# Moving the expert layers of two batches, a few loads and the tail of an mLSTM + mixture-of-depths kernel

## The chip, the cores and the metric

The kernel runs on one core of one Trainium2 chip. The metric is the device time of one execution in microseconds, lower is better. The engines are named as the profile names them: PE (matmuls, with its weight loads as PEld), DVE (vector), ACT (scalar, activations), POOL (GpSimd), and SP, which here only issues DMAs.

## What is computed

First an mLSTM cell over q, k, v of 4 batches, 8 heads, 768 tokens, 40 numbers per head. Its output, with the heads side by side, is x of 4 x 768 x 320, and goes into a mixture-of-depths layer: in each batch the 128 tokens with the highest scores go through two dense layers, the others pass unchanged.

```python
for t in range(S):                      # mLSTM, per batch and head
    m_new = np.maximum(f_gate[:, :, t] + m, i_gate[:, :, t])
    f_stab = np.exp(f_gate[:, :, t] + m - m_new)
    i_stab = np.exp(i_gate[:, :, t] - m_new)
    C = f_stab * C + i_stab * outer(vt, kt)
    n = f_stab * n + i_stab * kt
    y[:, :, t] = sigmoid(o_gate[:, :, t]) * (C @ qt) / max(abs(n @ qt), 1)
...
scores = np.einsum('bsd,d->bs', x, w_gate)
out = x.copy()
for b in range(B):                      # mixture of depths, capacity 128
    top_idx = np.argpartition(-scores[b], capacity)[:capacity]
    xe = x[b, top_idx]
    ye = np.maximum(xe @ w1, 0.0) @ w2  # 320 -> 1024 -> 320
    out[b, top_idx] = x[b, top_idx] + sigmoid(scores)[:, None] * ye
```

All of it is float32.

## The kernel before

The order of every engine's work is written out by hand in `_fast`; nothing is rescheduled, so each engine and each DMA queue does its instructions in the order of the program text. The sequence is cut into 12 steps n = 0 to 11: batch b = n // 3, and 256 tokens s = n % 3 of it. A step does the following.

- SP issues the loads of step n + 3 (`load`): v and k (`load_kv`, two DMAs of 160 KB each), q (one of 320 KB), and the output gate o of step n + 2 (`load_o`, four of 80 KB). The results of a step (x) are stored by `store`, two DMAs. The buffers of k, q and v go round by three. All of these DMAs are in one queue, SP's. Stores 0, 1, 2 are issued in step 4 and stores 3, 4 in step 5, between q and o of the loads; the weights w1 and w1c (the rows of w1 above 256) at the end of step 4's issues, w2 at the beginning of step 5's.
- `scores(n)` (line 297): 64 small matmuls k times q into the PSUM tile pS. `masked(n)` (line 303): DVE masks them into P.
- `fill` (line 562) repeats a dummy matmul twice, in steps 1 to 6.
- `widen(n+1)` (ACT, line 223) and `turn(n+1, "kT")`: PE transposes k of the next step (line 231), ACT copies it out of PSUM (line 233). `update(n+1)` (line 264) makes the contributions to the state C from k and the weighed v; `states` (DVE, lines 276 to 284) sums them. `weigh(n+2)` (POOL, line 243) multiplies v by the gates, two steps ahead.
- `read(n)` (line 319) multiplies q by the states; `turn(n+1, "qT")`; `attend(n)` (line 329) adds P times v. `divide(n)` (DVE, lines 338 to 343) makes y, `output(n)` (POOL, line 351) multiplies by the sigmoid of o into x, and `router(n)` (DVE, line 366) sums the scores of the tokens.

The mixture of depths runs between these. After a batch's last step, `spread` (line 394) lays all its scores along the free axis on all partitions; `ranks` counts for each token how many are greater, half by DVE (`greater`, line 406) and half by ACT (`signs`, line 411); `select` (DVE, line 445) makes a one-hot matrix of the ranks; `numbers` (PE, line 488) and `index` (DVE, lines 451 to 456) turn it into row numbers; `fetch` (POOL, line 494) gathers the 128 rows from `out` in HBM by an indirect DMA, so it waits until the stores of the batch have landed. `fetched` (PE, line 503) transposes the rows; `layer1` (lines 529 and 533, half of the 1024 columns per call, ReLU on ACT at line 535), `layer2` (line 545), `weighed` (ACT, line 550), and `add` (POOL, line 554), an indirect DMA that adds the result onto `out`.

In the kernel before, ranks and select of batch 0 are in step 5, with its fetch at the end of that step; `fetched(0)` and both halves of `layer1(0)` come at the end of step 6; `layer2(0)`, `weighed(0)` and `add(0)` in step 7. Batch 1 has ranks and fetch in step 7, `fetched` and `layer1` at the end of step 8, the rest in step 10. Batch 2 has ranks and fetch in step 10, `fetched` and its first half of layer1 in step 11, before `read`.

Batch 3 makes the tail. Its rows are not gathered from HBM: `picked` (lines 464 to 473) makes the one-hot matrix in float32, and PE multiplies x by it in three groups of columns (line 471). Four of the six score columns are compared early (`ranks_first`); the last two are spread by `spread(b, 4, 6, keep=True)`, which leaves them in PSUM, and compared there by DVE and ACT (`ranks_last`). `picked_numbers` (line 479) gets score, count and row number of the picked tokens by six float32 matmuls of 3 columns. A final matmul pg (line 678) sums flags that tell whether the fast path held.

PSUM is handed out in tiles by tag: "s" (pS, pB, a half of layer1) and pU each have one buffer of two banks, "h" (pH, pX) one, "t" (transposes, py, pi) two of one bank.

Of the kernel before, what the change touches and what calls it, by code (L numbers as in the profile page):

```python
# [9 lines left out]
FP = mybir.dt.float32  # L10
# [16 lines left out]
def _fast(ctx, tc, q, k, v, i_gate, f_gate, o_gate, w_gate, w1_in, w2_in, out):  # L27
# [49 lines left out]

    def load(n, between=()):

        if n < N:  # L80
            load_kv(n, v_t, v)
            load_kv(n, k_t, k)
            load_q(n)
        for i in between:
            store(i)
        if n <= N:
            load_o(n - 1)
# [199 lines left out]

    def scores(n):
        kT, qT = pending[n]["kT"], pending[n]["qT"]
        pS = ps_s.tile([128, 2, 2, NP, 64], FP, name="pS", tag="s")  # L290
        for c in range(2):
            for p in range(NP):
                for j in range(2):
                    for r in range(2):
                        e, o = slice(64 * j, 64 * j + D), slice(64 * r, 64 * r + 64)
                        t = slice(128 * c + 64 * r, 128 * c + 64 * r + 64)
                        PE.matmul(pS[o, j, c, p, :], kT[e, p, t], qT[e, p, t], start=True, stop=True)  # L297
        pending[n]["pS"] = pS
# [89 lines left out]

    def spread(b, r0, r1, keep=False):

# [5 lines left out]
        flat = pB.rearrange("p j t -> p (j t)")[:, 0:128 * w]  # L396
        if keep:
            return flat
        sb = mod.tile([128, 128 * w], FP, name=f"sb{w}", bufs=1)
# [28 lines left out]
    def ranks_last(b):  # L428
# [7 lines left out]
        DVE.tensor_scalar(out=part[:, 4:6], in0=part[:, 4:6], scalar1=0.5 * 255, scalar2=None, op0=OP.add)  # L436
        sb = spread(b, 4, 6, keep=True)
        for r in range(6):
# [20 lines left out]
    def picked(b):  # L459
# [7 lines left out]
        for j, pX in enumerate((ps_u.tile([128, 2, 512], FP, name="pU"), ps_h.tile([128, 2, 512], FP, name="pX", tag="h"),  # L467
                                ps_t.tile([128, 1, 512], FP, name="pX", tag="t"))):
            w = min(128, DM - 128 * j)
            for r in range(2 * NS):  # L470
                PE.matmul(pX[0:w, 0, 0:128], x[:, r, 128 * j:128 * j + w], sel[:, r, :], start=(r == 0), stop=(r == 2 * NS - 1))
            ACT.copy(out=d["xeT"][0:w, j], in_=pX[0:w, 0, 0:128])
        DVE.tensor_copy(out=d["xeT"][64:128, 2], in_=pX[0:64, 0, 0:128])

    def picked_numbers(b):
        x, d = x_t[b % 2], dep[b]
        pi = ps_t.tile([128, 3], FP, name="pi", tag="t")
        for r in range(2 * NS):
            PE.matmul(pi, d["sel_f"][:, r, :], x[:, r, DM:DM + 3], start=(r == 0), stop=(r == 2 * NS - 1))
        d["g"] = mod.tile([128, 1], FP, name="g")  # L480
# [34 lines left out]
    def layer1(b, f0):  # L515
# [5 lines left out]
        early, last = b < B - 2, b == B - 1  # L521
        if (early and f0 == 0) or (last and f0 > 0):
            ph = ps_s.tile([128, 2, 512], FP, name="ph", tag="s")
        else:
            ph = ps_u.tile([128, 2, 512], FP, name="pU")
# [54 lines left out]
    for n in range(N):  # L580
# [3 lines left out]
        given = late or n == 5  # L584
        if n == 5:
            SP.dma_start(out=w2, in_=w2_in.rearrange("(f p) d -> p f d", p=128))
        if n in (6, 9):
            store(n - 1)
        if n > 0:
            load(n + 3, {4: (0, 1, 2), 5: (3, 4)}.get(n, ()))  # L590
        if n == 4:
            SP.dma_start(out=w1, in_=w1_in[0:256, :].rearrange("(j p) f -> p j f", j=2))
            for i in range(2):
                SP.dma_start(out=w1c[64 * i:64 * i + 64],
                             in_=w1_in[256:DM, :].rearrange("p (f i e) -> p i f e", i=2, e=128)[:, i])
        if n in (7, 8, 10, 11):
            store(n - 1)
        scores(n)
        masked(n)
        if n == 0:  # L600
            update(0)
            load(3)
            states(0)
        if 0 < n < 7:
            fill(spare(n + 1)[:, 0], 2)
        if late:
            layer2(b - 2)
        if given:
            ranks(b - 1)
            select(b - 1)  # L610
        if late:
            weighed(b - 2)
        if n > 0 and (s == 0 or late or not more):
# [9 lines left out]
        if not more:  # L623
            sigmoid(n)
            gated(n)
            fetched(b - 1)
            layer1(b - 1, 0)
        read(n)
        if late:
            numbers(b - 1, spare(n + 1)[:, 1, 0:3])  # L630
        if n + 2 < N:
            weigh(n + 2)
        if late:
            fetch(b - 1)
        if n == 0:
            update(1)
            states(1)
        if more:
            turn(n + 1, "qT")
            sigmoid(n)  # L640
            if b > 0 and s == 0:
                dep[b - 1] = {"sb": spread(b - 1, 0, 2 * NS)}
        else:
            dep[b] = {"sb4": spread(b, 0, 4)}
            ranks_first(b)
        attend(n)
# [3 lines left out]
        if more:  # L650
            output(n)
        if n == 5:
            fetch(b - 1)
        if late:
            add(b - 2)
        if n == 0:
            tables()
        if n == 1:
            margins()
        if n in (6, 8):  # L660
            fetched(n // 4 - 1)
            layer1(n // 4 - 1, 0)
            layer1(n // 4 - 1, 4)
    b = B - 1
# [4 lines left out]
    store(N - 1)  # L669
    layer2(b - 1)  # L670
    picked(b)
    picked_numbers(b)
    weighed(b - 1)
    layer1(b, 0)
    add(b - 1)
    good = gate.tile([1, 1], I32, name="good")
# [362 lines left out]
```

## Time and profile before

| what | value |
|---|---|
| time, median of 4 runs | 178.08 us (176.32 to 179.85) |
| the profiled execution's own time | 176.32 us |
| its span, first to last instruction | 174.5 us |
| PE busy / weight loads | 150.6 us (86%) / 130.8 us (75%) |
| DVE, ACT, POOL busy | 92.8, 73.9, 68.8 us |
| granted TensorE clock, mean | 0.970 |
| DMA | 24.14 MB in 94104 packets, 88401 of them under 512 bytes |
| SP's queue | 69.2% of 16 engines' span |
| chain that ended last | PE 51%, DMA 18%, DVE 9%, issue 7%, POOL 6% |

The span is cut in the page into 40 slices of 4.36 us, with the busy share of each engine in tenths. A row of the timeline or of the chain begins with its start in us from the span's start and its length; `x16` is the number of instructions merged into it, and a bracket tells how long the engine was idle before it and what released it. The steps begin (first matmul of `scores`) at 12.91, 21.53, 28.74, 37.03, 46.02, 53.30, 62.72, 85.48, 97.31, 111.32, 119.44 and 131.26 us.

### The profile page before, as it was taken

What the parts mean: (1) busy time and instruction counts of PE and PEld (TensorE: products, weight loads), DVE (VectorE), ACT (ScalarE), POOL (GpSimd) and SP (SyncE); (2) the same over time, 40 slices, a digit from 0 to 9 for tenths busy, and PEclk for the clock granted to TensorE, in tenths of its full rate; (3) what the DMA queues carried; (4) which work ended last, traced back from release to release, by engine and by line L of the source; (5) the groups of instructions that cost most, each with busy time, mean ns of one, the idle gap of its engine ahead of it and who ended that gap; (6) DMA issues with size and microseconds to landing.
All of it is one profiled execution on the core that took longest, in us unless ns stands there. A gap on an engine that the chain in (4) does not pass through costs nothing.

```text
span 174.5 us, 6700 instructions
## 1 busy us (share of the span) xinstructions
PE 150.6 (86%) x2877; PEld 130.8 (75%) x2877; DVE 92.8 (53%) x252; ACT 73.9 (42%) x140; POOL 68.8 (39%) x89
## 2 busy tenths in 40 slices
PE   7969999899996978819999988999995999889930
PEld 7859899688985866808868977898694987678710
DVE  4676466486567996321196475185958756210000
ACT  0668464345459433320554553449343193121110
POOL 8045476745545336200721935671124712003030
PEclk9999999999999999996999999999999999996995
DMA  6999888898999789699989999997821603003003
GB/s 104 191 164 187 163 139 152 140 175 133 154 164 169 123 154 260 126 374 305 227 190 178 162 171 187 203 140 151 159 53 41 116 0 75 6 0 38 11 8 41
DMA packets 94104, 24.14 MB, mean 138 GB/s; under 512 B 88401, under 2 KB 93714, under 8 KB 94066
## 3 DMA queue, kind: packets, MB, share of 16 engines
q1 hardware_dynamic: 93104, 22.32, 69.2%
q0 software_dynamic: 720, 1.15, 4.1%
q8 instruction: 24, 0.39, 0.9%
q10 hardware_dynamic: 242, 0.17, 0.5%
q14 instruction: 14, 0.11, 0.2%
HBM read 19.04 MB, written 4.59 MB: 135 GB/s over the span
## 4 chain that ended last, share of the span: by engine, by line
PE 51%; DMA 18%; DVE 9%; issue 7%; POOL 6%; ACT 3%; ACTq 1%; SPq 1%; POOLq 0%; DVEq 0%
PE pt L231 8%; PE pU L264 7%; DMA xe<-out_dram,idx 6%; PE pH L329 5%; PE py L545 5%; DMA v<-in_v_dram 5%; PE pH L319 5%; PE pS L297 4%; PE pU L529 3%; PE ph L529 3%; POOL wv L243 3%; DMA k<-in_k_dram 3%; DMA out_dram<-yg,idx 2%; PE pB L394 2%; DMA i_sb<-in_i_gate_dram 2%
## 5 line engine op out<-in xcount | busy, mean ns | idle before, releaser
L243 POOL TENSOR_TENSOR wv<-v,cols 64x656 f32<-64x656 f32 x23 | 31.2, 1357 | 51.9 <-DMA v<-in_v_dram 47.4
L351 POOL TENSOR_TENSOR x<-y,o 128x320 f32<-128x320 f32 x24 | 20.5, 873 | 13.2 <-DVE x L384 5.0
L303 DVE TENSOR_TENSOR P<-pS,mask 128x1024 f32<-128x1024 f32 x12 | 14.6, 1217 | 13.9 <-PE pS L297 13.0
L235 ACT COPY qT<-pt 128x512 f32<-128x512 f32 x24 | 13.9, 633 | 18.6 <-PE pt L231 18.6
L545 PE MATMUL py<-w,hT 128*128 128x320 f32 x64 | 18.2, 437 | 0.0
L223 ACT COPY qw<-q 128x640 f32<-128x640 f32 x12 | 8.7, 722 | 21.5 <-DMA q<-in_q_dram 19.2
L231 PE MATMUL pt<-ident,k 128*128 128x128 f32 x96 | 14.2, 282 | 3.7 <-DMA k<-in_k_dram 3.1
L264 PE MATMUL pU<-wv,k 128*64 128x82 f32 x384 | 16.5, 237 | 0.1
L276 DVE TENSOR_TENSOR C<-pU,C 128x164 f32<-128x164 f32 x40 | 13.1, 328 | 6.6 <-PE pU L264 5.5
L329 PE MATMUL pH<-wv,P 128*64 128x82 f32 x384 | 16.3, 237 | 0.0
L554 POOL DMA_INDIRECT out_dram<-yg,idx x4 | 6.4, 1603 | 24.4 <-ACT yg L550 21.4
L264 PEld LDWEIGHTS pU<-wv,k 128*64 128x64 f32 x384 | 14.4, 137 | 2.1 <-issue 1.6
L366 DVE CUSTOM_DVE_ANT_0 scr<-x,wg 128x320 f32<-128x320 f32 x22 | 13.6, 616 | 4.2 <-POOL x L351 2.6
L329 PEld LDWEIGHTS pH<-wv,P 128*64 128x64 f32 x384 | 14.3, 136 | 1.8 <-issue 1.0
L231 PEld LDWEIGHTS pt<-ident,k 128*128 128x128 f32 x96 | 11.1, 145 | 5.8 <-PE pt L231 1.7
L545 PEld LDWEIGHTS py<-w,hT 128*128 128x128 f32 x64 | 11.8, 190 | 4.7
L319 PE MATMUL pH<-C,qT 40*64 40x41 f32 x704 | 14.0, 229 | 0.7 <-issue 0.7
L297 PE MATMUL pS<-qT,kT 40*64 40x64 f32 x768 | 13.9, 221 | 0.7 <-ACT qT L235 0.7
L319 PEld LDWEIGHTS pH<-C,qT 40*64 40x64 f32 x704 | 12.5, 134 | 2.0 <-issue 1.0
L297 PEld LDWEIGHTS pS<-qT,kT 40*64 40x64 f32 x768 | 12.3, 134 | 2.0 <-ACT qT L235 0.9
L233 ACT COPY kT<-pt 128x512 f32<-128x512 f32 x24 | 12.8, 586 | 1.8 <-PE pt L231 1.8
L231 PE MATMUL pt<-ident,qw 128*128 128x128 f32 x96 | 13.2, 279 | 0.4 <-DVE cols L216 0.4
(136 smaller groups left out, 223.5 us busy)
## 6 DMA issues: line engine op xcount, KB each, us to landing
k<-in_k_dram SPq DMA_DIRECT2D x24, 160.0 KB, 5.0
q<-in_q_dram SPq DMA_DIRECT2D x12, 320.0 KB, 5.7
v<-in_v_dram SPq DMA_DIRECT2D x24, 160.0 KB, 4.1
o<-in_o_gate_dram SPq DMA_DIRECT2D x48, 80.0 KB, 3.8
out_dram<-x SPq DMA_DIRECT2D x24, 160.0 KB, 2.8
w<-in_moe_w_dram SPq DMA_DIRECT2D x1, 1280.0 KB, 8.1
w<-in_moe_w_dram SPq DMA_DIRECT2D x1, 1024.0 KB
w1c<-in_moe_w_dram SPq DMA_DIRECT2D x2, 128.0 KB
```

The source lines that it names most:

```text
L231: PE.transpose(pt[:, p, :], src[:, c, 2 * p:2 * p + 2, :].rearrange("s j d -> s (j d)"), ident)
L235: ACT.copy(out=T.rearrange("e p (u t) -> e t p u", t=2)[:, c], in_=pt)
L243: (DVE if n == 0 and r else POOL).tensor_tensor(out=wv_t[n % 3][o, :, :, r], in0=v_t[n % NB][o], op=OP.mult, in1=cols[s][o, 0:2, b * H:b * ...
L264: PE.matmul(pU[64 * j:64 * j + 64, c, p], k_t[n % NB][:, c, 2 * p + j, :], wv_t[n % 3][:, c, 2 * p + j], start=True, stop=True)
L276: DVE.tensor_tensor(out=C, in0=src, in1=state[n, i], op=OP.add)
L297: PE.matmul(pS[o, j, c, p, :], kT[e, p, t], qT[e, p, t], start=True, stop=True)
L303: DVE.tensor_tensor(out=P.rearrange(flat), in0=pending[n].pop("pS").rearrange(flat), op=OP.mult, in1=mask.unsqueeze(1).to_broadcast([128, ...
L319: PE.matmul(g["pH"][64 * c:64 * c + 64, NP * j + p, r], g["qT"][e, p, t], state[n, 2 * c + r][e, p, :], start=(c, j) not in g["begun"], st ...
L329: PE.matmul(g["pH"][64 * c:64 * c + 64, NP * j + p], g["P"][:, j, c, p, :], wv_t[n % 3][:, c, 2 * p + j], start=(c, j) not in g["begun"], ...
L351: POOL.tensor_tensor(out=x.rearrange(order, j=2, d=D), in0=pending[n]["y"][:, r].rearrange("s (j p) d -> s j p d", j=2), in1=o.rearrange(o ...
L366: DVE.tensor_tensor_reduce(out=scr, in0=x[:, r, 0:DM], in1=wg, scale=1.0, scalar=0.0, op0=OP.mult, op1=OP.add, accum_out=x[:, r, DM:DM + 1])
L545: PE.matmul(d["py"], d["hT"][:, f, :], w2[:, f, :], start=(f == 0), stop=(f == NF - 1))
```

## The change

- Loads: store 0 goes to step 4, stores 1 and 2 into the loads of step 8 (step 5), behind v and k and ahead of q; w1 and w1c one step later, followed by stores 3 and 4; w2 one step later.
- Batches 0 and 1: `fetch(0)` moves from step 5 to step 6, behind `output`; `fetch(1)` stays in step 7 but behind `output(7)`, and `weigh(9)` comes behind it. `fetched` of both moves into the middle of `scores` of steps 8 and 9, `layer1` of both behind `masked` of those steps; `layer2(0)`, `weighed(0)` and `add(0)` from step 7 to step 8. The two halves of `layer1` of these batches change PSUM tiles. Step 7 gets a `fill`.
- Step 11: `fetched(2)` behind `read`, `layer1(2, 0)` behind `spread`.
- Tail: the last two score columns are copied to SBUF by ACT before they are compared; `picked` carries the three extra columns of x (score, count, row number) along in its third group of matmuls, and `picked_numbers` becomes one transpose of 3 partitions; `weighed(2)` and `add(2)` move up, and `layer1(3, 0)` comes ahead of `picked_numbers`.

```diff
-    def load(n, between=()):
+    def load(n):
         if n < N:
             load_kv(n, v_t, v)
             load_kv(n, k_t, k)
+            if n == 8:
+                store(1)
+                store(2)
             load_q(n)
-        for i in between:
-            store(i)
+        if n == 7:
+            store(0)
         if n <= N:
             load_o(n - 1)
...
-    def scores(n):
+    def scores(n, between=None):
...
         for c in range(2):
+            if c == 1 and between is not None:
+                between()
             for p in range(NP):
...
-    def spread(b, r0, r1, keep=False):
+    def spread(b, r0, r1):
...
-        if keep:
-            return flat
         sb = mod.tile([128, 128 * w], FP, name=f"sb{w}", bufs=1)
         ACT.copy(out=sb, in_=flat)
         return sb
...
-        sb = spread(b, 4, 6, keep=True)
+        sb = spread(b, 4, 6)
...
-            w = min(128, DM - 128 * j)
+            w = min(128, XW - 128 * j)
             for r in range(2 * NS):
                 PE.matmul(pX[0:w, 0, 0:128], x[:, r, 128 * j:128 * j + w], sel[:, r, :], start=(r == 0), stop=(r == 2 * NS - 1))
+            w = min(128, DM - 128 * j)
             ACT.copy(out=d["xeT"][0:w, j], in_=pX[0:w, 0, 0:128])
         DVE.tensor_copy(out=d["xeT"][64:128, 2], in_=pX[0:64, 0, 0:128])
+        d["three"] = mod.tile([128, 128], FP, name="three", bufs=1)
+        DVE.tensor_copy(out=d["three"][64:XW - 256], in_=pX[64:XW - 256, 0, 0:128])
     def picked_numbers(b):
-        x, d = x_t[b % 2], dep[b]
+        d, e = dep[b], slice(64, XW - 256)
         pi = ps_t.tile([128, 3], FP, name="pi", tag="t")
-        for r in range(2 * NS):
-            PE.matmul(pi, d["sel_f"][:, r, :], x[:, r, DM:DM + 3], start=(r == 0), stop=(r == 2 * NS - 1))
+        PE.transpose(pi, d["three"][e], ident[e, e])
...
-        if (early and f0 == 0) or (last and f0 > 0):
+        if (early and f0 > 0) or (last and f0 > 0):
             ph = ps_s.tile([128, 2, 512], FP, name="ph", tag="s")
...
-        if n == 5:
+        if n == 6:
             SP.dma_start(out=w2, in_=w2_in.rearrange("(f p) d -> p f d", p=128))
         if n in (6, 9):
             store(n - 1)
         if n > 0:
-            load(n + 3, {4: (0, 1, 2), 5: (3, 4)}.get(n, ()))
-        if n == 4:
+            load(n + 3)
+        if n == 5:
             SP.dma_start(out=w1, in_=w1_in[0:256, :].rearrange("(j p) f -> p j f", j=2))
...
+            store(3)
+            store(4)
...
-        scores(n)
+        scores(n, (lambda: fetched(n - 8)) if n in (8, 9) else None)
         masked(n)
...
-        if 0 < n < 7:
+        if 0 < n < 8:
             fill(spare(n + 1)[:, 0], 2)
-        if late:
-            layer2(b - 2)
+        if n in (8, 9):
+            layer1(n - 8, 0)
+            layer1(n - 8, 4)
+        if n in (8, 10):
+            layer2(n // 2 - 4)
...
-        if late:
-            weighed(b - 2)
+        if n in (8, 10):
+            weighed(n // 2 - 4)
...
             gated(n)
-            fetched(b - 1)
-            layer1(b - 1, 0)
         read(n)
...
-        if n + 2 < N:
+        if n + 2 < N and n != 7:
             weigh(n + 2)
-        if late:
-            fetch(b - 1)
+        if n == 10:
+            fetch(2)
...
         else:
+            fetched(b - 1)
             dep[b] = {"sb4": spread(b, 0, 4)}
+            layer1(b - 1, 0)
             ranks_first(b)
...
-        if n == 5:
-            fetch(b - 1)
-        if late:
-            add(b - 2)
+        if n in (6, 7):
+            fetch(n - 6)
+        if n == 7:
+            weigh(n + 2)
+        if n in (8, 10):
+            add(n // 2 - 4)
...
-        if n in (6, 8):
-            fetched(n // 4 - 1)
-            layer1(n // 4 - 1, 0)
-            layer1(n // 4 - 1, 4)
...
     layer2(b - 1)
+    weighed(b - 1)
     picked(b)
+    add(b - 1)
+    layer1(b, 0)
     picked_numbers(b)
-    weighed(b - 1)
-    layer1(b, 0)
-    add(b - 1)
```

## The prediction

> **What bounds the kernel now.** I read the page's slices first, then the chain of work that ended last, then the timeline around each long piece of that chain, with the SP queue beside it.
>
> The page's slices (4.36 us each) show what is scarce:
>
> ```profile
> PE   7969999899996978819999988999995999889930
> DVE  4676466486567996321196475185958756210000
> PEclk9999999999999999996999999999999999996995
> DMA  6999888898999789699989999997821603003003
> ```
>
> PE is full almost everywhere, and the DMA engines are full up to slice 27 (122 us): two resources are near their limit together. PE's hole is in slices 16 to 18, and its clock falls there and again in slice 36.
>
> The chain puts names on the holes (start, length, what ran):
>
> ```profile
> 71.41 6.09 DMA xe<-out_dram,idx
> ...
> 77.64 0.53 PE pX L503 x3
> ...
> 78.62 3.67 PE ph L529 x16
> ...
> 129.97 3.85 DMA xe<-out_dram,idx
> ...
> 154.56 1.51 PE pi L479 x12
> ```
>
> PE waits for the gather of batch 0 from 73.64 to 77.64, then runs layer1(0)'s first 16 matmuls in 3.67 us instead of the 2.05 of later ones. The chain holds few other waits of that size before the tail.
>
> The SP queue's timeline shows that it issues without a pause:
>
> ```profile
> 63.38 4.86 SPq L358 DMA_DIRECT2D out_dram<-x  x6
> 68.29 2.71 SPq L75 DMA_DIRECT2D o<-in_o_gate_dram  x4
> 71.04 1.26 SPq L592 DMA_DIRECT2D w<-in_moe_w_dram  x1
> 72.35 1.20 SPq L594 DMA_DIRECT2D w1c<-in_moe_w_dram  x2
> 73.59 0.69 SPq L586 DMA_DIRECT2D w<-in_moe_w_dram  x1
> 74.38 4.32 SPq L64 DMA_DIRECT2D v<-in_v_dram  x2
> ...
> 90.62 1.33 SPq L64 DMA_DIRECT2D v<-in_v_dram  x2
> ```
>
> v and k of step 8 leave at 74.38 to 82.24, behind six stores and both weights, and the loads of step 9 from 90.62. So a saving on PE is real only if the loads come as early.
>
> The tail, by the windows' rows (PE busy, PEld, DVE, ACT, POOL, granted clock, DMA):
>
> ```profile
> 154.00:156.00 2.00, 1.44 (x13) 1.44 (x13) 0.28 (x1) 0.19 (x1) 0.00 (x0) 1.00 0.00 0
> 156.00:158.00 2.00, 2.00 (x16) 2.00 (x16) 0.38 (x3) 0.59 (x2) 1.03 (x1) 0.82 0.00 0
> 158.00:160.00 2.00, 2.00 (x14) 1.51 (x13) 0.20 (x2) 0.34 (x1) 0.54 (x1) 0.50 0.48 37
> 160.00:162.00 2.00, 2.00 (x16) 2.00 (x15) 0.10 (x1) 0.25 (x1) 0.00 (x0) 0.83 0.31 53
> ```
>
> Right after the thin pi matmuls (3 columns each) the clock is halved for about 3.4 us (0.18, 0.50 and 0.17 of three 2 us windows are lost), while PE does layer1(3).
>
> **Part 1, batches 0 and 1 (steps 7 to 9).** Before, PE ends attend(6) at 73.64 and starts turn(10) at 112.42: 38.8 us. I rebuild this stretch with its own rows.
>
> Step 7, from 73.64: scores 1.09, fill 0.64 (new), turn k 1.02, update 1.28, read 1.07 give 78.7. Now numbers(1) needs DVE's select, and layer2(0), which gave it 4.5 us of cover, is gone: this is a new wait. DVE: y of step 6 ends at 75.21; from the start of P to the end of select took 5.34 us before (86.71 to 92.05), so select ends at 80.6 and PE stands about 2 us. Behind it wait turn q (1.02) and attend (1.29); with numbers 0.29, step 7 ends at 83.3. ACT meets the same time: widen(8) waits for q8 and the copies of turn k stand behind it. q8 now has two stores more in front, so it leaves near 74 and with the queue's median of 5.7 us lands at 79 to 80; that is level with select.
>
> The loads: SP ends q7's issue at 63.3. Store 0 takes 1.3, four o loads 2.7 to 4.1, v8 and k8 2.5 to 4, so k8 is issued by about 71.5 and lands (5.0) by 76, against a turn k at 75.4: 0 to 1 us, inside the 2 us wait above. Stores 1 and 2 land by about 77; fetch(0) goes at 77, after output(6), and takes 5.4 to 6.1 us: 82.5 to 83.2, in time for the transposes at 83.9. The 6 us gather is now under step 7.
>
> Step 8, from 83.3: scores with the three transposes inside 1.62, layer1 twice 2.05+0.65 less pipelining = 5.33, layer2 4.52: 94.8. The xeT copies (0.46 of PE idle before) lie under the second half of the scores. w1 leaves at 76 to 81; the nearest row is w2, 8.1 us to landing for more bytes, the low end a k load, 5.0: 81 to 89. I take 84, as w1 before was issued at 71.04 and in use by 78.62; it is needed at 84.9, so the bound of this cost is 0 to 4 us. The halves of layer1 change PSUM tiles: the second uses that of the scores, free after P (1.22), under the first half's 2.65; cost nothing, 1.2 without that cover.
>
> Then k9. The same items stand ahead of v9 in both orders (v8, k8, q8, o6, o7, stores 0 to 5, w1, w2), so the DMA work ahead of it is the same; only slack can go. The one slice below 8 there is slice 16 (69.8 to 74.2, "6"), some 1.7 us, and the six stores in a row left at SP's pace. I take 2 us; bounds 0 and 3. The second k9 load was issued at 93.1, now 91.1, and lands at 96.1 by the median 5.0. PE reaches it at 95.4 and stands 0.7. weigh(9) is now behind fetch(1) on POOL, and fetch(1) behind the landing of stores 3 to 5 (issued by 89, landed by 92): fetch 1.06 and weigh 2.6 end by 96, just under turn k. After k9: second half of turn 0.65, update 1.28, read 1.07, turn q 1.02, attend 1.29, and I keep the 0.67 us of unexplained idle in read(8): 102.1. Step 9: scores with transposes 1.62, layer1 5.33: turn(10) at 109.0. **Gain 3.4 us**; 1.4 with no slack, 4.1 with k9 no obstacle. Later loads move with v9 by the same 2 us and were early (k11 leaves at 111, is used at 125). add(0), 1.65 on POOL, and add(1) stay off the path.
>
> **Part 2, step 11.** Before, PE waited from 132.35 to 133.95 for the gather and 0.46 for the copies. Now read (1.07) and spread (1.09) come between. Next late is router(10): its scores are ready at 135.8, and half of spread's columns need them. PE then ends spread at 136.15, layer1 2.7, attend 1.3: 140.2 against 141.1. **Gain 0.9**; bounds 0.1 (all of spread waits) and 1.9 (no wait).
>
> **Part 3, the tail from the end of attend(11).** Before, 141.08 to the end of layer2(3) at 167.34: 26.3 us.
> Comparing from SBUF costs one ACT copy of 128x256 (0.37, L505's row; under 0.58, the row of 512 columns), under DVE's two 512-column comparisons (to 145.15); uncovered it would cost itself. ACT's three signs, which stood 2.61 us behind DVE's comparisons, now run beside them; a sign of 256 from SBUF lies between 0.47 and 0.72. Select is ready 1.7 us sooner, and PE's layer2(2) is late next, ending 7.57 us after attend (148.65 on the old scale) where picked began at 149.53. Picked takes 4.39; its 3 more columns ride in the third group. "three" is one small DVE copy (at most L473's 0.28), under layer1. layer1(3,0) then follows at once, since its first 16 matmuls need only copies already made: 2.70. pi is one transpose (between pg's 0.19 and the old 1.51; 0.2, it is nearest to pg), then a new wait: pg stands behind ACT's g and DVE's idx and flags, 0.75 (pi's end 156.06 to flags' end 156.72, and a semaphore), formerly under layer1; layer1(3,4) is queued behind it. pg 0.15, layer1 2.70, layer2 4.52. Sum 7.57+4.39+2.70+0.2+0.75+0.15+2.70+4.52 = 22.98. **Gain 3.3**, of which 1.7 is the halved clock, which I expect gone with pi's 1.5 us. Final weighed and add are unchanged, and add(2) moves away from them.
>
> The Trainium skill, "TensorE: Matmul & The Clock Gate" (Part 1), speaks against this last term: the clock halves after an idle window of about 3.4 us. Here PE was busy 1.44 of 2 us just ahead of the halving, with no gap over 0.9 us, so by that rule pi would not be the cause and might leave the slow stretch in place: the gain would be 1.6, not 3.3. I follow the row.
>
> **Sum.** 3.4 + 0.9 + 3.3 = 7.6 us. The profiled execution took 176.32 (span 174.5), so it becomes 168.7; it is the fastest of the four runs, 1.76 below their median of 178.08, and on that base the forecast is 170.5 us.
>
> **Rivals.**
> (a) The queue has no slack to give: part 1 gives 1.4 us when only k9 is late and about none with w1 at its late end; with 0.5 the total is 4.7, the time 173.4. For it: DMA at 9 in nearly all slices to 118 us. Against: slice 16.
> (b) The halved clock stays in the tail: 1.7 us back, 172.2. For it: pi's successor still breaks PE's stream by 0.95 us. Against: all else there becomes dense.
> (c) Both: 175.1 or a little more.
> (d) Slower than before: weigh(9) on POOL, queued behind fetch(1), which waits for stores 3 to 5, which stand behind w1 and partly w2. It is free up to 96; each us later is a us on update(9). It eats the whole gain at 103.6 and makes the kernel slower by over 1% from 105.4; at 107 the time is 181.5. For it: v8, issued just behind w2, was used only at 83.94, 9.6 us after its issue began. Against: stores needed 2.8 us to land.
>
> **Chances and range.** Forecast 0.47 (own range 168.3 to 172), (a) 0.21, (b) 0.15, (c) 0.08, (d) 0.09. About 1% is what a measurement here can tell. Faster: forecast, (a), (b) and a third of (c), 0.85; same: most of (c), 0.06; slower: (d), 0.09. The range runs from 167.5 (all three parts at their better bounds save one) to 176.0 and leaves out (d) and the ends.
>
> **What will show it.** Part 1: no gap of 4 us near step 6's end, full clock in all slices before 150 us; a gap of about 2 us at numbers(1) (L488) in step 7; v9 issued near 88.6. Part 2: spread ahead of layer1, waiting for the router. Part 3: sgn no longer released by cmp; layer1(3,0) right after picked; full clock to its end. I am wrong if the loads of step 9 land with PE long waiting, or if the clock falls again.

## The result, and the profile after

| | before | after |
|---|---|---|
| time, median | 178.29 us (32 runs) | 174.25 us (22 runs) |
| ratio | | 0.983, 95% interval 0.978 to 0.988 |
| the profiled execution | 176.32 us | 172.09 us |
| its span | 174.5 us | 170.4 us |
| scores(6) to the end of attend(6) | 10.9 us | 10.9 us |
| end of attend(6) to turn(10) | 38.8 us | 39.0 us |
| scores(11) to the end of the span | 43.2 us | 38.8 us |

The forecast was 170.5 us, a gain of 7.6 us; 4.0 us came. In this pair of profiles the third part of the change and the second gave what was forecast, and the first gave nothing. Ratios with an interval count only runs within 1.5% of a kernel's fastest, few of them where the runs spread over 5% as here; so medians over all runs stand beside them below, and differences of 1 us between two medians of six runs say little.

The page's slices after (4.26 us each, busy share in tenths):

```profile
PE   7969999999999795995699989999999799997920
DVE  5573584677566997569435008904894969511000
PEclk9995999999999999999569999999999999999995
DMA  6999978898889789989999799699861160330012
```

Against the slices of before, the hole in PE of slices 16 to 18 (counted from 0) is gone, and so is the 6 of PEclk in slice 36 (the tail). But a new hole stands in slices 18 and 19 with PEclk at 5 and 6 in 19 and 20: 81 to 88 us, steps 7 and 8.

What that hole is, PE's timeline of steps 7 and 8 after tells (start, length, line, operation, count, and in brackets the idle time before it with its releaser):

```profile
78.05 1.14 PE L324 MATMUL pH<-C,qT 40*64 40x41 f32 x64
82.58 0.30 PE L493 MATMUL pU<-place,sel 128*128 128x3 bf16 x6 [3.39 <-DVE C L279]
82.75 1.95 PE L234 MATMUL pt<-ident,qw 128*128 128x128 f32 x8
84.62 2.46 PE L334 MATMUL pH<-wv,P 128*64 128x82 f32 x32
87.01 1.14 PE L302 MATMUL pS<-qT,kT 40*64 40x64 f32 x32
```

PE stands 3.39 us at numbers(1). The releaser isn't select: it is C, the sums that `states` makes of pU. The same engine's rows show the queue that PE waits through; this is DVE's timeline of that stretch:

```profile
79.55 0.96 DVE L448 TENSOR_TENSOR sel<-iota,cnt 128x768 bf16<-128x768 f32 x1
80.43 0.48 DVE L371 CUSTOM_DVE_ANT_0 scr<-x,wg 128x320 f32<-128x320 f32 x1
...
81.48 1.05 DVE L279 TENSOR_TENSOR C<-pU,C 128x164 f32<-128x164 f32 x3
```

Select ends at 80.5, about where the prediction had it (80.6). Behind it stand router(6) and states(8), and numbers(1) writes into the tile pU that states(8) reads. From within the wait on, 81.47 to 88.29 us, the granted clock is halved by the trace's clock records: turn q takes 1.95 us instead of 1.09, attend 2.46 instead of 1.36, the first half of scores 1.14 instead of 0.69. Step 8 begins at 87.01 where the prediction had 83.3.

The chain of work after shows the second new wait, around step 9:

```profile
79.47 6.48 DMA w<-in_moe_w_dram
...
86.65 3.83 DMA out_dram<-x
90.48 3.95 issue
...
95.24 4.16 DMA xe<-out_dram,idx
...
99.56 1.30 POOL wv L246
...
100.90 1.35 PE pU L267 x32
```

Stores 3 and 4 leave behind w1 and store 5 behind w2, fetch(1) waits on POOL until they have landed, the second half of weigh(9) (99.56) starts only when the gather has landed, and update(9) follows it at once. The SP queue after:

```profile
81.47 2.68 SPq L363 DMA_DIRECT2D out_dram<-x  x4
84.19 1.07 SPq L591 DMA_DIRECT2D w<-in_moe_w_dram  x1
86.02 1.25 SPq L363 DMA_DIRECT2D out_dram<-x  x2
87.65 3.84 SPq L64 DMA_DIRECT2D v<-in_v_dram  x2
91.59 3.33 SPq L64 DMA_DIRECT2D k<-in_k_dram  x2
95.02 1.23 SPq L68 DMA_DIRECT2D q<-in_q_dram  x1
```

v9 leaves 3 us sooner than before (87.65 against 90.62), but it now stands behind w2 and store 5 alone, and its two issues take 3.84 us instead of 1.33, those of k9 3.33 instead of 1.77; q9 is later than before (95.02 against 93.91).

The tail before, three rows of PE's timeline:

```profile
149.53 1.58 PE L471 MATMUL pU<-sel_f,x 128*128 128x128 f32 x12 [0.87 <-DVE sel_f L464]
...
154.56 1.50 PE L479 MATMUL pi<-x,sel_f 128*128 128x3 f32 x12 [0.67 <-DVE xeT L473]
155.93 2.53 PE L529 MATMUL pU<-xeT,w 128*128 128x128 f32 x16
```

The tail after, from picked on:

```profile
147.74 1.50 PE L474 MATMUL pU<-sel_f,x 128*128 128x128 f32 x12
149.08 2.81 PE L474 MATMUL pX<-sel_f,x 128*128 128x128 f32 x24
151.73 1.95 PE L534 MATMUL pU<-xeT,w 128*128 128x128 f32 x16
153.61 0.71 PE L538 MATMUL pU<-xeT,w1c 64*128 64x128 f32 x8
154.26 0.22 PE L484 MATMUL pi<-ident,three 3*128 3x3 f32 x1
155.63 0.19 PE L686 MATMUL pg<-flags,ones 128*1 128x5 f32 x2 [1.15 <-DVE flags L459]
155.75 2.05 PE L534 MATMUL ph<-xeT,w 128*128 128x128 f32 x16
```

Picked starts without a wait (before, it stood 0.87 us for sel_f), layer1(3, 0) follows it, pi takes 0.22 instead of 1.50, and both halves of layer1 run at the full clock (1.95 and 2.05; before 2.53 and 2.54). The new wait ahead of pg is there, 1.15 us.

### The profile page after: what moved, and what is told of

The parts are those of the page before. It is cut to its first block, busy times and chain, and to the rows that moved or that the text cites. A ratio compares the mean times of both kernels' runs of the same rounds, so it can differ in the third digit from the quotient of the medians.

```text
span 170.4 us, 6692 instructions
## 1 busy us (share of the span) xinstructions
PE 149.9 (88%) x2870; PEld 130.7 (77%) x2870; DVE 94.4 (55%) x253; ACT 74.3 (44%) x141; POOL 69.5 (41%) x89
## 3 DMA queue, kind: packets, MB, share of 16 engines
q0 software_dynamic: 720, 1.15, 4.2%
## 4 chain that ended last, share of the span: by engine, by line
PE 56%; DMA 17%; issue 10%; DVE 5%; POOL 4%; ACT 2%; SPq 2%; ACTq 1%; POOLq 1%; DVEq 0%
PE pt L234 10%; PE pU L267 8%; PE pH L334 7%; DMA k<-in_k_dram 6%; PE pH L324 6%; PE py L550 5%; PE pU L534 4%; PE pS L302 4%; DMA w<-in_moe_w_dram 4%; PE pB L399 4%; DMA xe<-out_dram,idx 2%; DMA f_sb<-in_f_gate_dram 2%; DMA out_dram<-x 2%; POOL wv L246 2%; PE pX L474 2%
## 5 line engine op out<-in xcount | busy, mean ns | idle before, releaser
L246 POOL TENSOR_TENSOR wv<-v,cols 64x656 f32<-64x656 f32 x23 | 30.4, 1322 | 43.7 <-DMA v<-in_v_dram 26.2
L267 PE MATMUL pU<-wv,k 128*64 128x82 f32 x384 | 17.2, 245 | 1.1 <-POOL wv L246 1.0
L267 PEld LDWEIGHTS pU<-wv,k 128*64 128x64 f32 x384 | 15.2, 144 | 3.2 <-POOL wv L246 2.0
L334 PE MATMUL pH<-wv,P 128*64 128x82 f32 x384 | 17.4, 246 | 0.0
L334 PEld LDWEIGHTS pH<-wv,P 128*64 128x64 f32 x384 | 15.4, 143 | 2.0 <-issue 1.3
L302 PE MATMUL pS<-qT,kT 40*64 40x64 f32 x768 | 15.4, 231 | 0.7 <-ACT qT L238 0.7
L234 PE MATMUL pt<-ident,k 128*128 128x128 f32 x96 | 13.7, 277 | 1.9 <-DMA k<-in_k_dram 1.3
L302 PEld LDWEIGHTS pS<-qT,kT 40*64 40x64 f32 x768 | 13.4, 143 | 2.4 <-ACT qT L238 0.9
L234 PE MATMUL pt<-ident,qw 128*128 128x128 f32 x96 | 14.1, 292 | 0.4 <-DVE cols L219 0.4
L324 PEld LDWEIGHTS pH<-C,qT 40*64 40x64 f32 x704 | 12.4, 134 | 1.9 <-PE pS L302 0.8
```

The source lines that it names most:

```text
L234: PE.transpose(pt[:, p, :], src[:, c, 2 * p:2 * p + 2, :].rearrange("s j d -> s (j d)"), ident)
L246: (DVE if n == 0 and r else POOL).tensor_tensor(out=wv_t[n % 3][o, :, :, r], in0=v_t[n % NB][o], op=OP.mult, in1=cols[s][o, 0:2, b * H:b * ...
L267: PE.matmul(pU[64 * j:64 * j + 64, c, p], k_t[n % NB][:, c, 2 * p + j, :], wv_t[n % 3][:, c, 2 * p + j], start=True, stop=True)
L324: PE.matmul(g["pH"][64 * c:64 * c + 64, NP * j + p, r], g["qT"][e, p, t], state[n, 2 * c + r][e, p, :], start=(c, j) not in g["begun"], st ...
L334: PE.matmul(g["pH"][64 * c:64 * c + 64, NP * j + p], g["P"][:, j, c, p, :], wv_t[n % 3][:, c, 2 * p + j], start=(c, j) not in g["begun"], ...
```

## The experiments

All times are medians over all runs of a kernel, beside the median of before in the same comparison. The theory at the outset: the tail gives its 4 us; the head (the loads and the layers of batches 0 and 1) gives nothing because of the new wait at numbers(1). The rivals: the halved clock behind it; weigh(9) behind fetch(1); the queue, with DMA engines that are full; the tail's gain an accident of one profile's clock.

### Taking the new waits away: e1, e2, e3

e1 puts numbers(1) behind attend(7), e2 puts weigh(9) ahead of fetch(1), e3 does both.

```diff
-        if late:
+        if late and n != 7:
             numbers(b - 1, spare(n + 1)[:, 1, 0:3])
...
-        if n == 5:
+        if n in (5, 7):
             numbers(b - 1, spare(n + 1)[:, 1, 0:3])
...
-        if n in (6, 7):
-            fetch(n - 6)
         if n == 7:
             weigh(n + 2)
+        if n in (6, 7):
+            fetch(n - 6)
```

> The changed kernel with numbers(1) of step 7 moved from behind read to behind divide, as step 5 has it, so that PE no longer stands there for select, router and states. Theory A (the stand of 3.4 us at numbers(1) and the clock halved behind it, 81.5 to 88.3, ate the gain of the first part): PE goes through step 7 without a gap over 1 us, the clock stays full, and the time falls by 2.5 to 4 us against the changed kernel, to about 171. Theory B (the loads of step 9 and weigh(9) behind the landing of fetch(1) are the limit, and PE's stand only fills time that it would wait later): the gap and the slow clock go just the same, but update(9) still starts near 100.5 to 101, PE stands in front of it 3 us or more, and the time falls by less than 0.8 us.

> The changed kernel with weigh(9) ahead of fetch(1) on POOL in step 7. Its second half then no longer waits for fetch(1) to land. Theory A: nothing, since PE comes late to update(9) anyway: at most 0.4 us (the idle before update(9) in the profile). Theory B: weigh(9) ends near 98.5 instead of 100.9, and by itself also only 0.3 to 0.5 us, since PE comes at 100.6. What tells them apart is the next kernel with both edits.

> Both edits: numbers(1) behind divide and weigh(9) ahead of fetch(1). Theory A: as numbers(1) late alone, 2.5 to 4 us faster than the changed kernel. Theory B: 1 to 2 us faster than the changed kernel: weigh(9) is out of the way, and then the second k load of step 9 (landing near 99) holds the second half of turn k at about 99.

Before was at 178.62. e1: 176.58 us, slower than the changed kernel. The wait at numbers(1) was gone, another took its place in e1's timeline of PE:

```profile
85.70 1.97 PE L234 MATMUL pt<-ident,qw 128*128 128x128 f32 x8 [2.83 <-ACT kT L236]
```

turn q waits for ACT's copies of turn k, which stand behind widen(8), and that waits for q8, as ACT's timeline of e1 shows; the prediction had called it "level with select":

```profile
84.44 0.73 ACT L226 COPY qw<-q 128x640 f32<-128x640 f32 x1 [4.56 <-DMA q<-in_q_dram]
85.07 1.06 ACT L236 COPY kT<-pt 128x512 f32<-128x512 f32 x2
```

The clock is halved behind this wait too (84.8 to 95.1 us). e2: 173.73, which six runs can't tell from the changed kernel. e3: 173.98; from the end of attend(6) to turn(10) its profile has 34 us instead of 39, but its step 6 ended 6.6 us later (attend(6) ended at 80.3 us, after: 73.7), so the time didn't show it. So numbers(1) alone, theory A of e1, falls; e3 needed more runs.

### The two parts by themselves: e4, e11, e5, e15, and before again: b2

e4 and e11 are one kernel: before, with step 11 and the tail of the change. e5 and e15: the change, with step 11 and the tail of before.

The core of the first against before:

```diff
+            fetched(b - 1)
             dep[b] = {"sb4": spread(b, 0, 4)}
+            layer1(b - 1, 0)
             ranks_first(b)
...
-        sb = spread(b, 4, 6, keep=True)
+        sb = spread(b, 4, 6)
...
-            PE.matmul(pi, d["sel_f"][:, r, :], x[:, r, DM:DM + 3], start=(r == 0), stop=(r == 2 * NS - 1))
+        PE.transpose(pi, d["three"][e], ident[e, e])
```

e5 undoes the same lines in the changed kernel.

> The kernel before with only the new order of step 11 and the new tail. By the two profiles the end of attend(11) comes 1.1 us and the tail from there 3.6 us sooner, so 4 to 5 us faster than the kernel before, that is the whole gain of the change or a little more, if (as I read the traces) steps 6 to 9 gave nothing. If instead the first part did help and the tail gave less, this kernel gains only 1.5 to 2.5 us.

> The change's loads and its layers of batches 0 and 1 alone; step 11 and the tail are those of before. Theory A (the halves add up by the medians: whole change 4.0 us, tail and step 11 alone 1.8 us): the head is worth about 2.2 us, 176 us or 1.2% under before. Theory B (what the first pair of profiles says: turn(10) starts at 112.69 after against 112.42 before, so the head gives nothing): within 0.5 us of before. Both expect the wait of 3 to 4 us at numbers(1) in step 7 and v9 issued near 87.6 us. A segment from scores(11) to the span's end near 43 us would say that the old tail is dear in itself, one near 41 us that its halved clock window in the profile of before was an accident of that execution.

> The kernel before once more, for a second profile of it. If the halved clock window in layer1(3) follows from the thin matmuls of pi, it is there again and scores(11) to the end takes 43 us; if it was an accident of the first execution, this stretch is about 41.5 us. The idle stretch of 4 us near step 6's end with its half clock should be there in both cases, and attend(6)'s end to turn(10) near 38.8 us.

> The same kernel as e4_tail_only, step 11 and the tail alone, in more rounds. The stretch from scores(11) to the span's end is 42.4 to 43.2 us in three profiles with the old tail and 38.4 to 39.0 in seven with the new one. Theory A (the tail is worth those 4.1 us, and the head nothing): 174 to 175 us. Theory B (the first run of it was right, the tail is worth 1.8 us by the times): about 176.8.

> e5_head_only once more. Theory A (the head is worth nothing): within 0.7 us of before. Theory B (head and tail add up to the whole, the tail being worth 2 us by the times): 176 to 176.8 us. Step 11 to the end 42 to 43 us in both.

| | time | before beside it | scores(11) to the end |
|---|---|---|---|
| e4, tail alone | 176.79 | 178.62 | 38.7 us |
| e11, the same | 176.35 | 178.09 | 39.0 us |
| e5, head alone | 178.86 | 179.07 | 42.4 us |
| e15, the same | 179.26 | 178.02 | 42.5 us |
| b2, before | 179.88 (one run) | | 42.9 us |

By the times the head alone is worth nothing: 0.2 us faster once, 1.2 slower once. The tail's rows are as steady as anything here: over 5 profiles with the old tail the stretch takes 42.4 to 43.2 us (mean 42.7), over 15 with the new one 38.2 to 39.0 (mean 38.6): 4.1 us, where the prediction had 4.2. So the first profile was no accident. In all five old tails the halved clock begins about 1 us behind pi, as in PE's timeline of e15:

```profile
157.19 1.50 PE L484 MATMUL pi<-x,sel_f 128*128 128x3 f32 x12 [0.67 <-DVE xeT L478]
158.55 2.86 PE L534 MATMUL pU<-xeT,w 128*128 128x128 f32 x16
```

and its windows (PE, PEld, DVE, ACT, POOL busy, then the granted clock and DMA) show it at about one half from 159.5 to 163:

```profile
157.00:159.00 2.00, 1.81 (x16) 1.81 (x17) 0.20 (x2) 0.27 (x2) 0.00 (x0) 1.00 0.00 0
159.00:161.00 2.00, 2.00 (x15) 2.00 (x13) 0.31 (x3) 0.32 (x1) 1.40 (x1) 0.64 0.00 0
161.00:163.00 2.00, 2.00 (x14) 1.51 (x14) 0.24 (x2) 0.39 (x1) 0.17 (x1) 0.51 0.68 71
```

In none of the 15 new tails is the clock halved before the last layer2's end. One thing doesn't fit: by the times the tail alone is worth 1.8 us (twice), not 4.1, and the parts add up to less than the whole. The profiles don't settle it: with the tail alone scores(11) begins at 136.3 and 134.6 us, in the two of before at 131.3 and 135.1. This stays open.

### The halved clock of steps 7 and 8: e6

```diff
+        if n == 7:
+            fill(ps_s.tile([128, 2, 512], FP, name="pB", tag="s")[:, 0, 0:128], 10)
         if late:
             numbers(b - 1, spare(n + 1)[:, 1, 0:3])
```

> The changed kernel with ten dummy matmuls of 128 columns more between read(7) and numbers(1), so that PE is busy over most of the wait; the wait for DVE itself stays. Theory A (the clock is halved because PE stood still 3.4 us at numbers(1), and the halved clock is a cost of its own): no halved stretch in step 7's second half and step 8's beginning, turn q near 1.1 us instead of 1.95, attend 1.3 to 1.4 instead of 2.46, 1 to 2 us faster than the changed kernel where nothing else is late. Theory B (what is won there is lost again to the second k9 load): the clock full in step 7 and step 8, a longer wait before the second half of turn(9), time within 0.5 us of the changed kernel.

175.58 us beside 179.07. Step 7 went as theory A has it: 11.5 us from scores(7) to scores(8) instead of 13.4, turn q 1.07 and attend 1.36 by the timeline's rows, no halved window there. The time didn't follow: in this profile two halved windows fell into step 6 (69.2 to 76.0 us), whose fill had waited 3.18 us for DVE, and attend(6) ended at 80.6. So theory A is right on the clock, which stays where PE is kept busy, but the gain that it forecast was not measured: the 12 runs have a mean of 175.4 us, the changed kernel 174.6 over all its runs.

### The queue and the load: e7, e8, e9, e10

e7 puts loads of step 9 ahead of w2 (on e3):

```diff
+            if n == 9:
+                SP.dma_start(out=w2, in_=w2_in.rearrange("(f p) d -> p f d", p=128))
+                store(3)
+                store(4)
+                store(5)
+            load_q(n)
             if n == 8:
                 store(1)
                 store(2)
-            load_q(n)
...
-        if n == 6:
-            SP.dma_start(out=w2, in_=w2_in.rearrange("(f p) d -> p f d", p=128))
-        if n in (6, 9):
+        if n == 9:
             store(n - 1)
...
-            store(3)
-            store(4)
```

> The changed kernel with numbers(1) put behind attend(7), weigh(9) ahead of fetch(1), and another order in SP's queue: q8 ahead of stores 1 and 2, and w2 and stores 3 to 5 behind v9 and k9, ahead of q9. Theory A (the loads of step 9 are late because they stand behind w2's 1.3 MB): v9 is issued 4 to 6 us sooner than in the changed kernel against step 7's beginning, the second k9 load has landed before PE reaches turn(9), no wait there, and the time is 1 to 3 us under the changed kernel. Theory B (the DMA engines are full, what is moved forward pushes something else back): w2, fetch(1) or q9 is late instead, in step 8 or 9, and the time is within 0.7 us of the changed kernel or above it.

176.47 us beside 179.07: theory B, what is moved forward pushes something back. v9 leaves at 84.64, but fetch(0) lands late and PE's timeline of e7 shows it:

```profile
89.55 0.87 PE L513 MATMUL pX<-ident,xe 128*128 128x128 f32 x3 [3.89 <-DMA xe<-out_dram,idx]
```

Is it then the load itself? e8 (after), e9 (e3) and e10 (before) leave out 7/8 of w2 and so move 1.15 MB less:

```diff
+    POOL.memset(w2[:, 1:, :], 0.0)
...
-            SP.dma_start(out=w2, in_=w2_in.rearrange("(f p) d -> p f d", p=128))
+            SP.dma_start(out=w2[:, 0, :], in_=w2_in[0:128, :])
```

> The changed kernel with 7/8 of w2 left out: those rows are zeros set by POOL in its idle time before 11 us, and the DMA moves 0.16 MB instead of 1.31 MB, so the rows that are added to out are not the reference's. Theory A (the queue between v7 and q9 moves the same bytes in 36.8 us, give or take 0.7, in whatever order, and steps 8 and 9 can't come sooner): q9 is issued 5 to 7 us sooner after v7 than before, stores 5, fetch(1) and weigh(9) come sooner, and the time is 2 to 4 us under the changed kernel's 174.25. Theory B (it is PE's own waits for DVE in steps 6 and 7 and the halved clock behind them that hold the head): the loads come sooner, PE doesn't, and the time is within 0.7 us of 174.25.

> As e3_both (numbers(1) behind attend(7), weigh(9) ahead of fetch(1)), with 7/8 of w2 left out as in e8_light_after. Theory A (the loads are the floor under the removed waits): what e3_both could not cash in comes now: 3 to 5 us under its 174.0, and more than e8_light_after gains. Theory B (waits and clock): as e3_both, within 0.7 us of 174.0. If e8 gains and e9 gains no more than e8, the waits were worth nothing.

> The kernel before with 7/8 of w2 left out in the same way. There step 6's end waits for the gather of batch 0, whose stores are issued ahead of w2, so the light queue shouldn't bring step 7 sooner; the second k9 load had landed at about 98.1 us with PE there at 98.4. Theory A (both kernels are at the loads' floor): 0 to 2 us under before, less than the changed kernel gains. Theory B (waits of PE alone): within 0.7 us of before.

Beside 178.09 of before: e8 174.04, e9 173.10, e10 181.53 us. The theory that the loads are the floor falls: with a twentieth of all bytes gone just ahead of step 9, the changed kernel is where it was (the wait at numbers(1) is 3.93 us in it), and before is no faster; that it was 3.4 us slower was not followed up. The queue is full, but it wasn't what held the head.

### Step 6, and the version that beats both: e12 to e17

e13 and e16 are e3 again, e14 is the changed kernel again, e12 and e17 are e3 with PE kept busy ahead of step 6's fill:

```diff
         masked(n)
+        if n == 6:
+            fill(ps_t.tile([128, 128], FP, name="pc6", tag="t"), 7)
```

> As e3_both, with seven dummy matmuls of 128 columns more behind scores(6), which run while PE would stand 1.6 to 4.3 us for DVE's flags ahead of step 6's fill. Theory A (the halved clock behind this wait is a cost of its own): no halved window between step 6's fill and step 7, and 1 to 2 us under e3_both in the same comparison. Theory B (the wait for DVE's chain of steps 5 and 6 itself is the cost, and the clock falls at the next wait instead): within 0.7 us of e3_both.

> e3_both once more, to stand beside the changed kernel on the same chip. If the removed waits are worth what steps 7 to 9 showed in its profile (34.1 us from attend(6)'s end to turn(10), against 39.1), it is 3 us or more under the changed kernel; if they are taken back elsewhere, within 0.7 us.

> The changed kernel once more: 174.3 us as before, step 11 to the end in 38.4 to 39.0 us, a wait of 3.4 to 3.9 us at numbers(1).

> e3_both a third time. If its two removed waits are worth about what steps 7 to 9 lost, its mean over all runs is 1 to 2 us under the changed kernel's 174.6; if not, 174 to 175 us. In the profile attend(6) ends anywhere from 73.5 to 80.5 us, by how many halved windows fall into step 6, at about 1.7 us each.

> e12_both_cover6 once more. Theory A (PE's wait for DVE's flags in step 6 starts the halved windows that lengthen step 6): no halved window between 63 us and the end of attend(6), and 1 us or more under e16_both_third. Theory B (the wait is the cost, not the clock): within 0.7 us of it.

| | time | before beside it | ratio, 95% interval |
|---|---|---|---|
| e14, the changed kernel | 175.32 | 178.02 | 1.000, 0.993 to 1.008 |
| e13, e3 again | 171.94 | 178.02 | 0.965, 0.956 to 0.973 |
| e16, e3 again | 171.56 | 177.60 | 0.977, 0.968 to 0.986 |
| e12, with cover | 174.70 | 178.02 | 0.964, 0.957 to 0.971 |
| e17, with cover | 173.68 | 177.60 | 0.986, 0.977 to 0.996 |

The ratios rest on a few runs of each kernel and don't order these as the medians do: by them e14 is no faster than before, and e12 is as fast as e13. Over all runs the means are 178.4 (before, 111 runs, standard error 0.2), 174.6 (changed, 34 runs, 0.2) and 172.8 (e3, 18 runs, 0.5): without its two new waits the change gives 5.6 us instead of 3.8. So they were worth 1.8 us, give or take 0.5; in the one comparison that has both, e13 is 3.4 us under e14. How much of it is either wait's the runs don't tell: the six runs of e1 have a mean of 177.0, those of e2 173.9. In e16 PE's timeline of step 7 comes near to what the prediction had forecast for it, one wait, of 1 us where it had 2, and the full clock:

```profile
81.91 1.14 PE L234 MATMUL pt<-ident,qw 128*128 128x128 f32 x8 [0.98 <-ACT kT L236]
82.98 1.36 PE L334 MATMUL pH<-wv,P 128*64 128x82 f32 x32
84.28 0.30 PE L493 MATMUL pU<-place,sel 128*128 128x3 bf16 x6
84.51 0.69 PE L302 MATMUL pS<-qT,kT 40*64 40x64 f32 x32
```

Where the rest of the head's gain may have gone, and one reason why runs of one kernel lie 5 us apart, e14 shows, the changed kernel a second time, in step 6:

```profile
69.60 1.20 PE L567 MATMUL pU<-hot 128*128 128x128 f32 x4 [3.18 <-DVE flags L459]
70.59 1.91 PE L234 MATMUL pt<-ident,k 128*128 128x128 f32 x8
72.43 2.46 PE L267 MATMUL pU<-wv,k 128*64 128x82 f32 x32
```

Step 6's fill waits for DVE's flags (1.64 us in the first profile after), and the clock is halved behind it. From scores(6) to the end of attend(6) the profiles take

| halved windows in step 6 | profiles | scores(6) to attend(6)'s end, mean |
|---|---|---|
| 0 | 4 with the old head, 4 with the new (2 of them e12 and e17) | 10.4 and 10.9 us |
| 1 | 1 old, 6 new | 12.7 and 12.4 us |
| 2 | 3 new | 14.8 us |
| 3 | 2 new | 15.6 us |

Four of five old heads have none; without a cover, 11 of 13 new ones have one or more. In those four old heads PE's wait is split, 1.3 to 1.6 us for k in step 5 and 0.9 to 1.2 us at this fill; the fifth (e10) has 0.8 and 2.1 us and a halved window. In the new ones it is 0 to 1.3 us for k and 1.4 to 4.3 us at the fill. Why k came earlier against PE there, no run tells. And in the old head a long step 6 could come out of a wait: PE then stood 2.5 to 5.8 us for the gather of batch 0. With the gather gone, the end of step 6 sets what follows, and without a cover attend(6) ends at 77.3 us on average, 74.8 in the old heads.

The cover of e12 and e17 did in step 6 what theory A said: no halved window between 63 us and the end of attend(6), which came at 73.3 and 73.8 us. It didn't make the kernel faster than e3 (174.70 and 173.68 against 171.94 and 171.56): in e17 PE then waits 2.15 us at turn q in step 7, and the clock is halved from 80.7 to 94.4. The waits move on, and the cover is 1.8 us of PE's time whether DVE is late or not. So that the halved windows of step 6 are what the times lack is not shown.

## Why the prediction was wrong, and where it was right

**Part 3, right.** Forecast 3.3 us, 3.6 from profile to profile (26.3 us to 22.6), and hardly different in the others: 26.3 to 26.4 us in the five profiles with the old tail, 22.6 in all 15 with the new. Select sooner, picked at once, pi one transpose of 0.22 (forecast 0.2), layer1(3, 0) ahead of it. The wait ahead of pg is 1.15 where 0.75 was forecast. The halved clock went with pi's thin matmuls: 5 of 5 profiles with them have it, 0 of 15 without. Rival (b) falls, and with it the rule that the prediction set against its own row: the Trainium skill, "TensorE: Matmul & The Clock Gate" (Part 1), ties the halving to an idle window; here PE had 0.67 us of idle time in the 3.41 us before it. No kernel changes pi alone: its wait of 0.67 us and the order behind it went with it.

**Part 2, right in the first pair of profiles, and by luck.** Forecast 0.9, found 1.0 (scores(11) to the end of attend(11): 9.8 us to 8.8). But the step "PE waited from 132.35 to 133.95 for the gather" took a term from one profile. PE's timelines of before and of its second profile, b2:

```profile
133.95 0.52 PE L503 MATMUL pX<-ident,xe 128*128 128x128 f32 x3 [1.53 <-DMA xe<-out_dram,idx]
...
136.94 0.52 PE L503 MATMUL pX<-ident,xe 128*128 128x128 f32 x3 [0.67 <-DMA xe<-out_dram,idx]
```

In the four other profiles with the old order the wait is 0.63 to 0.69 us and the stretch 9.0 to 9.1, in the 15 with the new order the stretch is 8.7 to 8.9: part 2 was worth 1.0 us in one pair and 0.2 to 0.3 us elsewhere.

**Part 1, wrong: 3.4 us forecast, none found in the times (e5, e15).** The step that failed first is "PE stands about 2 us" at numbers(1). It was priced for select alone, and select came when forecast. But numbers(1) writes the tile that states(8) reads, so it waits for all that DVE has queued up to there, router(6) and states(8), 2 us more; 3.0 to 3.9 us in the profiles. The row was there to be read, in the chain of before:

```profile
86.64 4.52 PE py L545 x16
...
94.48 0.34 DVE C L276
...
94.87 0.29 PE pU L488 x6
```

numbers(1) (L488) followed the last C sum there too, and layer2(0)'s 4.52 us stood in front. The second step that failed is "full clock in all slices before 150 us": a wait of 2 us was put into the sum at its own length, with no thought of what it does to the clock. The halved clock took the rest: turn q, attend and the first scores lost 2.4 us by their rows (1.95, 2.46, 1.14 against 1.09, 1.36, 0.69). Step 8 was to begin at 83.3 and began at 87.01. From there to turn(10) the forecast had 25.7 us (83.3 to 109.0) and the profile has 25.7 (87.01 to 112.69), so in this profile the whole miss lies in step 7.

Two further steps failed and cost next to nothing here. The third is "fetch 1.06 and weigh 2.6 end by 96": weigh(9) ended at 100.9, rival (d) in a mild form; update(9) waited 0.34 us for it. The fourth is the 2 us that k9 was to come sooner: v9 left 3 us sooner, and w2's backlog fell on it. That is rival (a), true in the trace, but not what held the time, as the light queue of e8 shows; that the measured 174.25 lies beside its 173.4 is chance.

Taking both waits away gave 1.8 us back. The remainder of the 3.4 shows in the profiles as step 6, whose length the prediction took as a constant 10.9 us from one profile; it varies from 9.6 to 15.7, and the gather's wait, which the change removed, had covered that. In the times this is not shown, since the cover of e12 and e17 gave nothing.

**The base.** The sum was set on a median of 178.08 by adding the difference to one profile; the median held (177.6 to 179.1 in later comparisons). But the profile of before was a short one where part 1 lies. From the end of attend(6) to turn(10) the five profiles with the old head take 38.8 to 43.9 us, mean 41.5, and 38.8 is the one that was used; the four with the change's head as it is (after, e5, e14, e15) take 37.8 to 39.1, mean 38.6, and the three of e3 33.6 to 35.4, where the forecast had 35.4. So against the mean this stretch did become 2.9 us shorter, while step 6 before it grew from 10.9 to 12.5; from scores(6) to turn(10) the means are 52.4, 51.1 and, in e3, 48.8 us. With so few profiles these are sizes, not proofs.

## What to carry to other kernels

When a wait is removed, ask what it covered: an engine that stood for a transfer also absorbed every late piece in front of it, and those are on the path as soon as the transfer isn't. An instruction that writes a shared tile waits for everything that its last reader has queued in front of that read, so read the releaser's whole queue, not the one input that is in mind. Price a new PE wait at its length plus a halved window behind it when PE is idle for 1.75 us or more within 3.41, and at an even chance of one from 1.25 us on, as the counts below have it. And look at several profiles before a stretch's length, or a wait's, is taken as a constant.

## What the runs showed of the hardware

The clock is granted in windows of 3.41 us whose phase differs between executions: ahead of the last 12 us every halved stretch in the records lasts 3.41 us or a multiple of it, and they begin at other times in each profile. Over 20 profiles (their start and last 12 us left out), a window at full clock in which PE was idle for 1.75 us or more in all was followed by a halved one in 25 of 25 cases, with 1.25 to 1.75 us in 10 of 19, and with less in 5 of 715, all five being the old tail's pi (matmuls of 3 columns). The Trainium skill, "TensorE: Matmul & The Clock Gate" (Part 1), gives the window's length and its free phase, which agree, and a whole idle window as the trigger, which doesn't: half a window was enough.

A DVE instruction that begins beside a POOL instruction can stand still for it. In e14 DVE's row `scr` took 1.59 us where its twin takes 0.48:

```profile
65.26 0.48 DVE L371 CUSTOM_DVE_ANT_0 scr<-x,wg 128x320 f32<-128x320 f32 x1
...
65.90 1.59 DVE L371 CUSTOM_DVE_ANT_0 scr<-x,wg 128x320 f32<-128x320 f32 x1
```

and POOL's timeline of the same stretch has weigh(7) from 65.86 on, two instructions of 1.3 us:

```profile
65.86 2.78 POOL L246 TENSOR_TENSOR wv<-v,cols 64x656 f32<-64x656 f32 x2 [5.53 <-DMA v<-in_v_dram]
```

The same shows beside weigh(7) in e3 (1.44 us in a row of C that elsewhere takes 0.33, and 1.60 in `scr`), e6 (1.58) and e15 (1.41); it puts 1 to 2 us on DVE's chain of step 6, and these are the profiles in which PE waits 3.0 us or more at the fill. Over all 20 profiles the 332 rows of `scr` with no POOL multiplication beside them take 0.51 us at most; the 89 that take over 0.75 us all have one beside them and end 0.34 to 0.36 us after its end. So the row lasts as long as POOL's instruction does; that POOL is the cause is still read from the traces, as no kernel took it apart.
